# Two weight chunks of an attention + mixer kernel, converted in eighths in turns 4 to 11 instead of whole in turn 0

## The chip, the cores and the metric

The kernel runs on 1 core of one Trainium2 chip. The metric is the device time of one execution in microseconds (us); lower is better.

## The reference, cut to what matters

```python
scores = scale * np.matmul(q, k.transpose(0, 1, 3, 2)) + bias     # 4 batches, 8 heads, 576 x 576, head size 64
attn = softmax(scores)
x = np.matmul(attn, v)                                            # gathered to 4 x 576 x 512
u = x + np.real(fft(fft(x, axis=1), axis=2))
un = (u - mean) / sqrt(var + 1e-6)
out = u + np.maximum(un @ w_ch1, 0.0) @ w_ch2                     # 512 -> 2048 -> 512
```

The bias is a small two-layer net of the relative position, one value for each head and pair of positions. The two weight matrices `w_ch1` and `w_ch2` arrive as 64-bit floats (read as pairs of 32-bit words), and the kernel makes 32-bit floats of them before the dense layers use them.

## The kernel before, in words

The work runs in three stages. The **bias stage** computes the bias, writes it through a ring of tiles to memory (`bias_d`) and to the bias tiles of the first pair of heads, and runs the scores of attention unit 0 between. The **attention stage** handles the other 15 units (4 pairs of heads x 4 batches) in a software pipeline of turns 0 to 14 and a tail. The **mixer stage** makes the Fourier sums and the dense layers.

In the attention stage the order of the work of PE, DVE and ACT is written out by hand in the table `ORDER`; each engine executes its share strictly in that order. The order of POOL and of SP, which issues nearly all transfers, is set by the scheduler of the framework, and is strict too. A turn goes through `ORDER` once (`turn_of`), for several units at a time: a step without a mark belongs to unit n in turn n, one mark (') to unit n-1, and so on. The letters: `S` nine score blocks on PE (two PSUM buffers), `D` the bias added and the row maximum found on DVE (L276), `X` the exponential on ACT (L284), `R` and `T` transposes of the probabilities on PE (L408 to L418, two PSUM buffers), `VR`, `VT` their copies to `pt` on ACT or DVE (L398, L400), `Q` the row sums (L454, L459), `A` the product with v (L439), `O`, `E`, `Y` the output's way to `x`. Steps of units below 0 do not exist, and S, D and X of unit 0 have been done in the bias stage, so turn 0 holds nothing but its weight steps.

The weight steps are `W0` to `W3` and `U0` to `U3`. `weights(n)` loads chunk n, one sixteenth, of either matrix with two transfers of 512 KB (`raw`, L152, one buffer each). `W0` (ACT, L154) copies the high words as floats to `wf`, scaled; `W1` (DVE, L155) keeps the sign, `W2` (L156) adds the three bits from the low words, `W3` (L157) joins them; then SP stores the 256 KB chunk to `w1_d[n]` (L528). `U0` to `U3` do the same for the second matrix (`uf`, `w2_d[n]`, L529). `raw` is free for the next chunk when W3 or U3 has read it. The dense layers read `w1_d` and `w2_d` long after. `prep` makes the high and low parts of q and k of the next unit on POOL (L196, L199) in eight pieces put between steps 4, 12, ... 60.

Of the kernel before, what the change touches and what calls it, by code (L numbers as in the profile page):

```python
# [9 lines left out]
F32 = mybir.dt.float32  # L10
# [10 lines left out]
P = 128  # L21
# [9 lines left out]
AHEAD = 19  # L31
HB = {"d": 8, "a": 6}
WHO = "ddda"
ON_ACT = set("R0 T00 T01 T03 T04 T10 T11 T12 T13".split())
N0 = 572
NT0 = N0 + S
# [8 lines left out]


ORDER = """
A3'' X8' A4'' S1 X2' X4' E1''' R1' D1 W0 S0 Y1''' R0' Q0' VR1' D0 T10' O'' S2 S4 Q1' D2 VR0' T00' VT10'
T01' VT00' D4 VT01' S3 T11' S6 T02' D3 D6 VT11' E2'' X3 S7 VT02' Y2'' S8 U0 T13' T12' A0' D7 X6 W1 VT13'
W2 W3 S5 T04' VT12' T03' D8 U1 A1' X7 X0 VT03' VT04' X1 D5 U2 U3 X5 A2'  # L50
""".split()

# [70 lines left out]
def body(ctx, tc, a, out):  # L123
    nc = tc.nc

    def pool(name, bufs, space=None, reuse="tile", stack=ctx, **kw):
        if space is not None:
            kw["space"] = space
        return stack.enter_context(tc.tile_pool(name=name, bufs=bufs, reuse_waits=reuse, **kw))
# [10 lines left out]
    w1_d = dram.tile([NF, P, 4, P], F32, name="w1_d")  # L140
    w2_d = dram.tile([NF, P, DM], F32, name="w2_d")
# [4 lines left out]
    def widen(src, dst, shape, rp):  # L146
        raw = rp.tile(shape, I64, tag="raw", name="raw")
        flat = raw.rearrange("p a b -> p (a b)") if len(shape) == 3 else raw
        words = flat.bitcast(I32).rearrange("p (n t) -> p n t", t=2)
        lo, hi = words[:, :, 0], words[:, :, 1]  # L150
        m = dst.bitcast(I32)
        nc.sync.dma_start(raw, src)  # L152
        return [
            lambda: nc.scalar.activation(dst, hi.bitcast(F32), AF.Copy, scale=2.0 ** -112),  # L154
            lambda: nc.vector.tensor_scalar(hi, hi, -0x80000000, None, ALU.bitwise_and),  # L155
            lambda: nc.vector.scalar_tensor_tensor(hi, lo, 29, hi, ALU.logical_shift_right, ALU.bitwise_or),  # L156
            lambda: nc.vector.scalar_tensor_tensor(m, m, 3, hi, ALU.logical_shift_left, ALU.bitwise_or),  # L157
        ]
# [3 lines left out]
    early_, late = ExitStack(), ExitStack()  # L162
# [25 lines left out]
    def prep(n):  # L188
        q, k = ld.pop(n)
        qs = stp.tile([P, 2 * S], F32R, tag="qs", name="qs")  # L190
        kh = stp.tile([P, KW], F32R, tag="kh", name="kh")
        kl = stp.tile([P, KW], F32R, tag="kl", name="kl")
        stk[n] = (qs, kh, kl)

        def hi(dst, src, c):
            nc.gpsimd.tensor_scalar(dst[:, c], src[:, c], 1.0, 0.0, ALU.mult, ALU.add)  # L196

        def lo(dst, src, ref, rows, c):
            nc.gpsimd.tensor_tensor(dst[rows, c], src[rows, c], ref[rows, c].bitcast(F32), ALU.subtract)  # L199

        every, low = slice(0, 128), slice(64, 128)
        ca, cb, ck = slice(0, S), slice(S, 2 * S), slice(S, KW)
        return [
            lambda: hi(qs, q, ca), lambda: lo(qs, q, qs, low, ca),
            lambda: hi(kh, k, ca), lambda: lo(kl, k, kh, every, ca),
            lambda: hi(qs, q, cb), lambda: lo(qs, q, qs, low, cb),
            lambda: hi(kh, k, ck), lambda: lo(kl, k, kh, every, ck),
        ]
# [72 lines left out]
    def expo(n, i):  # L281
        blk = (BLK if n else BLK0)[i]
        p = prob(n, blk)
        nc.scalar.activation(  # L284
            p, p, AF.Exp, bias=nms[n][:, blk:blk + 1], scale=-1.0, accum_out=sums[n][:, blk:blk + 1])
# [6 lines left out]
    with ExitStack() as st:  # L292
# [46 lines left out]
        def hidden(n):  # L339
            u, t4, _, low, _ = steps[n]  # L340
            col = lt[:, 4 * u + t4:4 * u + t4 + 1]
            off = NT0 if low is None else N0 - low
            src = tw[:, off:off + S]
            who = WHO[n % len(WHO)]
            h = hpool.tile([P, S], F32, tag="h" + who, name="h" + who, bufs=HB[who])
            if who == "a":
                nc.scalar.activation(h, src, AF.Relu, bias=col)
            else:
                nc.vector.tensor_scalar(h, src, col, 0.0, ALU.add, ALU.max)
            return h  # L350

        for n, (u, t4, rev, low, _) in enumerate(steps):
            for k in range(n, min(n + AHEAD, len(steps))):
                if k not in ahead and (k <= n + 2 or WHO[k % len(WHO)] != "d"):
                    ahead[k] = hidden(k)
# [27 lines left out]
    with ExitStack() as st:  # L383
        ptp = pool("ptp", 1, stack=late, side="right")
        otp = pool("otp", 2, stack=late, side="right")
        rawu = pool("rawu", 1, stack=late, side="right")
        tps = pool("tps", 2, PSUM, stack=st)
        ops = pool("ops", 1, PSUM, stack=st)
        score_ps = ExitStack()
# [32 lines left out]
        def turned(u, w, on_act):  # L422
            if u not in pts:
                pts[u] = ptp.tile([P, 9, S], F32, tag="pt", name="pt")
            pt, tp = pts[u], tp_.pop((u, w))
            if w == "R0":
                evac(pt[:, 0:8, 512:576].rearrange("p (j h) r -> p j h r", h=2), tp, on_act)
            elif w == "R1":
                for e in half:
                    evac(pt[e, 8, 512:576], tp[e, e], on_act)  # L430
            else:
                evac(pt[:, 2 * int(w[2]) + int(w[1]), 0:512], tp, on_act)

        def value(u, j):
            if j == 0:
                os_[u] = ops.tile([P, 2, 512], F32, tag="o", name="o")
            for c in range(2):
                for h, e in enumerate(half):
                    nc.tensor.matmul(  # L439
                        os_[u][e, c, :CH], vt[u][:, j, e], pts[u][:, 2 * j + h if j < 4 else 8, c * CH:(c + 1) * CH],  # L440
                        start=j == 0, stop=j == 4, tile_position=(0, e.start), skip_group_check=True,
                    )
            if j == 4:
                del pts[u], vt[u]
                if u + 2 < U:
                    load_v(u + 2)

        def out_a(u):
            ots[u] = otp.tile([P, S], F32, tag="ot", name="ot")
            nc.scalar.activation(ots[u].rearrange("p (c s) -> p c s", c=2), os_.pop(u)[:, :, :CH], AF.Copy)  # L450
# [26 lines left out]
        def scaled(u, w):  # L477
# [13 lines left out]
            "X": lambda u, w: expo(u, int(w[1])),  # L491
            "T": turn, "R": turn, "V": lambda u, w: turned(u, w[1:], w[1:] in ON_ACT),
            "A": lambda u, w: value(u, int(w[1])), "O": lambda u, w: out_a(u),
# [13 lines left out]
        def turn_of(n, between):  # L507

            for i, w in enumerate(ORDER):
                w, u = w.rstrip("'"), n - w.count("'")  # L510
                if w[0] in "WU":
                    wd(w)
                elif 0 <= u < U and (u or w[0] not in "SDX"):
                    steps[w[0]](u, w)
                for piece in between.pop(i, ()):
                    piece()
            assert not between
# [4 lines left out]
        def weights(n):  # L522

            wf = rawp.tile([P, 512], F32, tag="wf", name="wf")
            uf = rawu.tile([P, DM], F32, tag="wf", name="uf")
            w = widen(a["m1"][:, P * n:P * n + P].rearrange("(k p) c -> p k c", p=P), wf, [P, 4, P], rawp)
            u = widen(a["m2"][P * n:P * n + P], uf, [P, DM], rawu)
            w.append(lambda: nc.sync.dma_start(w1_d[n].rearrange("p k c -> p (k c)"), wf))  # L528
            u.append(lambda: nc.sync.dma_start(w2_d[n], uf))  # L529

            def step(name):
                todo = w if name[0] == "W" else u
                todo[int(name[1])]()
                if name[1] == "3":
                    todo[4]()
            return step

        for n in range(U - 1):
            pr = prep(n + 1) if n else []
            wd = weights(n)  # L540
            turn_of(n, {4 + 8 * i: [piece] for i, piece in enumerate(pr)})
            if n + 2 < U:
                load(n + 2)
            if n == 6:
                fs = tabp.tile([P, 3, 2, 2, NK], F32R, tag="tab", name="fs")
                nc.gpsimd.tensor_copy(fs[0:1, 0, 0, 0, 0:1], vt[6][0:1, 0, 0:1])
                nc.gpsimd.dma_start(fs, a["fs"])
# [197 lines left out]
        n = U - 1  # L745
        wd = weights(n)
# [45 lines left out]
        for w in TAIL:  # L792
            u = n - w.count("'")
            on_act = w in TAIL_ACT
            w = w.rstrip("'")
# [96 lines left out]
        for b in range(B):  # L892
# [3 lines left out]
            main, last_down, end = dense(ut, tl, store)  # L896
            if b + 1 < B:
                tl, un, pcs = prepare(b + 1)
                n = 4
            else:  # L900
                un, stats, scales = norm(rest_tiles)
                pcs = stats + scales
                n = 2
# [8 lines left out]
        main, last_down, end = dense(ut, rest_tiles, store)  # L912
# [58 lines left out]
```

## Time and profile before

| | |
|---|---|
| three runs | 808.09, 809.91, 810.04 us; median 809.91 us |
| the profiled execution | 810.2 us, of which the span from first to last instruction is 808.4 us |
| busy time: PE, DVE, ACT, POOL | 765.9 (95%), 437.5 (54%), 430.8 (53%), 380.0 (47%) us |
| bias stage, attention turns with the tail, the rest | up to 74, up to 345, up to 808 us, about |
| a quiet attention turn | 16.08 us |

A row of a timeline gives start, duration, engine, line and operation, with outputs and inputs; in square brackets stands the time that the engine sat idle just before, and what it waited for. A row of windows gives the busy time of each engine in a stretch, the granted clock of TensorE as a share of its higher level (PEclk), the busy share of the 16 DMA engines and the rate that they moved. A row of the chain gives start, duration and what the end of the program hung on in that time.

### The profile page before, as it was taken

What the parts mean: (1) busy time and instruction counts of PE and PEld (TensorE: products, weight loads), DVE (VectorE), ACT (ScalarE), POOL (GpSimd) and SP (SyncE); (2) the same over time, 40 slices, a digit from 0 to 9 for tenths busy, and PEclk for the clock granted to TensorE, in tenths of its full rate; (3) what the DMA queues carried; (4) which work ended last, traced back from release to release, by engine and by line L of the source; (5) the groups of instructions that cost most, each with busy time, mean ns of one, the idle gap of its engine ahead of it and who ended that gap; (6) DMA issues with size and microseconds to landing.
All of it is one profiled execution on the core that took longest, in us unless ns stands there. A gap on an engine that the chain in (4) does not pass through costs nothing.

```text
span 808.4 us, 13104 instructions
## 1 busy us (share of the span) xinstructions
PE 765.9 (95%) x4786; PEld 620.6 (77%) x4786; DVE 437.5 (54%) x932; ACT 430.8 (53%) x884; POOL 380.0 (47%) x315
## 2 busy tenths in 40 slices
PE   3997599999999999997999999999999999999997
PEld 2464577878788887775788888888888888888896
DVE  5796587878778886867755141531417323111433
ACT  5596388778787888744333342333333333332453
POOL 5601255654475464346555534544345544444342
PEclk9899599999999999997999999999999999999999
DMA  6879669897967864152211121111210112111332
GB/s 159 246 257 316 198 172 263 263 275 216 289 201 208 257 205 136 54 182 92 65 40 40 53 91 40 41 53 41 89 53 27 53 53 92 53 48 43 118 92 65
DMA packets 57712, 105.81 MB, mean 131 GB/s; under 512 B 7857, under 2 KB 26417, under 8 KB 56241
## 3 DMA queue, kind: packets, MB, share of 16 engines
q1 hardware_dynamic: 56896, 101.64, 42.1%
q0 software_dynamic: 288, 3.02, 1.1%
q8 instruction: 37, 0.61, 0.3%
q10 hardware_dynamic: 464, 0.33, 0.1%
q14 instruction: 27, 0.21, 0.1%
HBM read 78.58 MB, written 23.72 MB: 127 GB/s over the span
## 4 chain that ended last, share of the span: by engine, by line
PE 79%; DMA 6%; DVE 5%; POOL 3%; ACT 2%; issue 2%; SPq 1%; ACTq 0%; DVEq 0%; POOLq 0%
PE acc L862 23%; PE hp L848 23%; PE s L258 8%; PE o L439 7%; PE t L418 6%; PE bps L368 5%; DMA raw<-m 3%; PE abp L643 2%; DMA kT<-kT 2%; PE zp L624 2%; DMA qT<-qT 1%; POOL qs L196 1%; DVE un L723 1%; PE ut L737 1%; POOL kl L199 1%
## 5 line engine op out<-in xcount | busy, mean ns | idle before, releaser
L854 DVE SCALAR_TENSOR_TENSOR hl<-hp,hh 128x512 fp32r<-128x512 f32 (+1 forms) x80 | 50.7, 635 | 231.7 <-ACT hh L853 231.7
L828 POOL TENSOR_TENSOR w1l<-w,w1h 128x512 fp32r<-128x512 f32 x80 | 106.2, 1328 | 106.4 <-ACT w1h L827 102.5
L828 POOL TENSOR_TENSOR w2l<-w2f,w2h 128x512 fp32r<-128x512 f32 x64 | 85.3, 1332 | 103.9 <-ACT w2h L827 103.6
L848 PE MATMUL hp<-uh,w1h 128*128 128x512 f32 (+1 forms) x320 | 119.0, 372 | 2.0 <-DVE hl L854 1.2
L848 PE MATMUL hp<-ul,w1h 128*128 128x512 f32 (+1 forms) x320 | 118.8, 371 | 0.7 <-DVE ul L740 0.7
L276 DVE CUSTOM_DVE_ANT_0 p<-s,bias 128x576 f32<-128x576 f32 x128 | 95.2, 753 | 44.1 <-PE s L258 41.3
L848 PE MATMUL hp<-uh,w1l 128*128 128x512 f32 (+1 forms) x320 | 118.5, 370 | 0.0
L827 ACT ACTIVATE w1h<-w 128x512 fp32r<-128x512 f32 x80 | 50.4, 631 | 124.1 <-PE hp L848 108.0
L827 ACT ACTIVATE w2h<-w2f 128x512 fp32r<-128x512 f32 x80 | 50.5, 632 | 120.9 <-POOL w1l L828 76.3
L862 PE MATMUL acc<-w2l,hh 128*128 128x512 f32 x288 | 112.4, 390 | 0.0
L862 PE MATMUL acc<-w2h,hh 128*128 128x512 f32 x288 | 111.5, 391 | 0.0
L258 PE MATMUL s<-kh,qs 128*128 128x288 f32 (+1 forms) x320 | 100.9, 334 | 9.1 <-POOL kh L196 6.7
L862 PE MATMUL acc<-w2h,hl 128*128 128x512 f32 x288 | 107.4, 391 | 0.0
L284 ACT ACTIVATE p<-p,nm 128x576 f32<-128x576 f32 x128 | 98.1, 771 | 3.0 <-DVE nm L276 1.9
L398 ACT ACTIVATE pt<-t 128x512 f32<-128x512 f32 x141 | 78.0, 594 | 35.7 <-PE t L418 24.9
L418 PE MATMUL t<-ident,p 128*128 128x128 f32 x576 | 82.0, 279 | 9.3 <-ACT pt L398 4.6
L258 PE MATMUL s<-kl,qs 128*128 128x288 f32 (+1 forms) x320 | 90.3, 300 | 0.0
L196 POOL TENSOR_SCALAR kh<-kT 128x576 fp32r<-128x576 f32 (+1 forms) x32 | 25.2, 805 | 132.0 <-PE s L258 116.4
L439 PE MATMUL o<-pt,v 128*64 128x288 f32 x640 | 85.3, 412 | 0.0
L258 PEld LDWEIGHTS s<-kh,qs 128*128 128x128 f32 (+1 forms) x320 | 60.0, 188 | 25.8 <-POOL kh L196 7.3
L418 PEld LDWEIGHTS t<-ident,p 128*128 128x128 f32 x576 | 68.0, 144 | 13.6 <-issue 6.6
L848 PEld LDWEIGHTS hp<-uh,w1h 128*128 128x128 f32 x320 | 60.8, 190 | 13.1 <-DVE hl L854 1.7
(130 smaller groups left out, 1409.8 us busy)
## 6 DMA issues: line engine op xcount, KB each, us to landing
w2f<-w_d SPq DMA_DIRECT2D x80, 256.0 KB, 2.6
raw<-m SPq DMA_DIRECT2D x32, 512.0 KB, 4.7
bias_d<-ring SPq DMA_DIRECT2D x9, 1152.0 KB, 6.0
kT<-kT SPq DMA_DIRECT2D x32, 304.0 KB, 4.7
qT<-qT SPq DMA_DIRECT2D x32, 288.0 KB, 4.5
bias<-bias_d SPq DMA_DIRECT2D x24, 288.0 KB, 5.7
v<-v SPq DMA_DIRECT2D x16, 320.0 KB, 5.0
out<-x SPq DMA_DIRECT2D x18, 256.0 KB, 2.6
```

What stands on the lines that cost most here:

```text
L258: nc.tensor.matmul(ps[:m, c, :CH], qs[:, c0:c0 + m], kk[:, k0 + c * CH:k0 + (c + 1) * CH], start=k == 0, stop=k == 1, skip_group_check=True)
L276: nc.vector.tensor_tensor_reduce(p, bank.pop((n, i))[:, :, :CH], bias, -0.125, 3.0e38, ALU.add, ALU.min, nms[n][:, blk:blk + 1])
L284: nc.scalar.activation(p, p, AF.Exp, bias=nms[n][:, blk:blk + 1], scale=-1.0, accum_out=sums[n][:, blk:blk + 1])
L368: nc.tensor.matmul(ps[32 * t4:32 * t4 + 32, c, :CH], w2[:, int(rev)], h[:, c * CH:(c + 1) * CH], start=True, stop=True, tile_position=(0, ...
L398: nc.scalar.activation(dst, src, AF.Copy)
L418: nc.tensor.transpose(tp[:, 128 * t:128 * t + 128], pb[t].rearrange("p h s -> p (h s)")[:, k0:k0 + 128], ident)
L439: nc.tensor.matmul(os_[u][e, c, :CH], vt[u][:, j, e], pts[u][:, 2 * j + h if j < 4 else 8, c * CH:(c + 1) * CH], start=j == 0, stop=j == 4 ...
L827: nc.scalar.activation(h, src, AF.Copy)
L828: eng.tensor_tensor(l, src, h.bitcast(F32), ALU.subtract)
L848: nc.tensor.matmul(ps[:, :N], (wh, wl)[wi][:, P * kb:P * kb + P], ut[ui][:, kb, :N], start=i == 0, stop=i == len(mm) - 1)
L854: nc.vector.scalar_tensor_tensor(hl[:, :N], ps[:, :N], 0.0, hh[:, :N].bitcast(F32), ALU.max, ALU.subtract)
L862: nc.tensor.matmul(acc[t], h[i][:, P * t:P * t + P], w[j], start=f == 0 and k == 0, stop=f == NF - 1 and k == 2)
```

## The change

Turn 0 makes no weight chunk. Chunk 0 of the first matrix is cut into four blocks of 128 rows, chunk 0 of the second into four blocks of 128 columns, and each of the turns 4 to 11 converts one such block of 128x128 in a pool of its own (`rawx`, one buffer): the copy on ACT after step 10, the three DVE steps after steps 30, 40 and 50, and behind the last a 64 KB store. Besides, `W0` moves in `ORDER` from place 9, ahead of `S0`, to place 44, behind `U0`, `T13'` and `T12'`.

```diff
+FIRST = range(4, 12)
 ORDER = """
-A3'' X8' A4'' S1 X2' X4' E1''' R1' D1 W0 S0 Y1''' R0' Q0' VR1' D0 T10' O'' S2 S4 Q1' D2 VR0' T00' VT10'
-T01' VT00' D4 VT01' S3 T11' S6 T02' D3 D6 VT11' E2'' X3 S7 VT02' Y2'' S8 U0 T13' T12' A0' D7 X6 W1 VT13'
+A3'' X8' A4'' S1 X2' X4' E1''' R1' D1 S0 Y1''' R0' Q0' VR1' D0 T10' O'' S2 S4 Q1' D2 VR0' T00' VT10'
+T01' VT00' D4 VT01' S3 T11' S6 T02' D3 D6 VT11' E2'' X3 S7 VT02' Y2'' S8 U0 T13' T12' W0 A0' D7 X6 W1 VT13'
 W2 W3 S5 T04' VT12' T03' D8 U1 A1' X7 X0 VT03' VT04' X1 D5 U2 U3 X5 A2'
 """.split()
...
+        rawx = pool("rawx", 1, stack=late, side="right")
...
                 if w[0] in "WU":
-                    wd(w)
+                    if n:
+                        wd(w)
...
+        def first_weights(i):
+            c = slice(P * (i % 4), P * (i % 4) + P)
+            wf = rawx.tile([P, P], F32, tag="wf", name="wx")
+            if i < 4:
+                res = widen(a["m1"][c, 0:P], wf, [P, P], rawx)
+                dst = w1_d[0][:, i]
+            else:
+                res = widen(a["m2"][0:P, c], wf, [P, P], rawx)
+                dst = w2_d[0][:, c]
+            last = res.pop()
+            def end():
+                last()
+                nc.sync.dma_start(dst, wf)
+            return res + [end]
...
-            wd = weights(n)
-            turn_of(n, {4 + 8 * i: [piece] for i, piece in enumerate(pr)})
+            if n:
+                wd = weights(n)
+            between = {4 + 8 * i: [piece] for i, piece in enumerate(pr)}
+            if n in FIRST:
+                for i, piece in zip((10, 30, 40, 50), first_weights(FIRST.index(n))):
+                    between[i] = [piece]
+            turn_of(n, between)
```

How the order of the instructions changes is shown at three places. The line numbers of the change are two or three higher than those of before.

The first place is ACT where the bias stage ends and turn 1 begins. `pr` is the last exponential of unit 0; the first `wf` and `uf` are chunk 0 in turn 0, the second `wf` is chunk 1 in turn 1; `rs` is `Q0'`, `128x8x64` is `VR0'`, and the four copies behind it begin with `VT10'`. Before:

```order
L284 ACTIVATE p,sm<-p,nm 128x576 x2
L284 ACTIVATE pr,sm<-pr,nm 128x576
L154 ACTIVATE wf<-raw 128x512
L154 ACTIVATE uf<-raw 128x512
L154 ACTIVATE wf<-raw 128x512
L454 ACTIVATE rs<-sm 128x9
L398 ACTIVATE pt<-t 128x8x64
L398 ACTIVATE pt<-t 128x512 x4
L284 ACTIVATE p,sm<-p,nm 128x576
L154 ACTIVATE uf<-raw 128x512
```

With the change:

```order
L286 ACTIVATE p,sm<-p,nm 128x576 x2
L286 ACTIVATE pr,sm<-pr,nm 128x576
L457 ACTIVATE rs<-sm 128x9
L401 ACTIVATE pt<-t 128x8x64
L401 ACTIVATE pt<-t 128x512 x4
L286 ACTIVATE p,sm<-p,nm 128x576
L156 ACTIVATE uf<-raw 128x512
L156 ACTIVATE wf<-raw 128x512
L286 ACTIVATE p,sm<-p,nm 128x576
```

Three copies of weights have left the place between the exponential and `Q0'`; the copy of chunk 1 now stands behind `uf`.

The second place is DVE at the same point: `pr,nm<-s,bias_r` is the last block of unit 0, the `p,nm` behind it is `D1` of turn 1, and the two copies of 64x64 are `VR1'`. Before:

```order
L276 ISA pr,nm<-s,bias_r 128x576
L276 ISA nm 128x1
L155 TENSOR_SCALAR raw<-raw 128x512
L156 SCALAR_TENSOR_TENSOR raw<-raw 128x512
L157 SCALAR_TENSOR_TENSOR wf<-wf,raw 128x512
L155 TENSOR_SCALAR raw<-raw 128x512
L156 SCALAR_TENSOR_TENSOR raw<-raw 128x512
L157 SCALAR_TENSOR_TENSOR uf<-uf,raw 128x512
L276 ISA p,nm<-s,bias 128x576
L276 ISA nm 128x1
L400 COPY pt<-t 64x64 x2
```

With the change:

```order
L278 ISA pr,nm<-s,bias_r 128x576
L278 ISA nm 128x1
L278 ISA p,nm<-s,bias 128x576
L278 ISA nm 128x1
L403 COPY pt<-t 64x64 x2
```

All six weight steps ahead of `D1` and `VR1'` are gone.

The third place is SP where the bias stage ends: `bias_r<-ring` are the three transfers that the last block of unit 0 needs. Before:

```order
L329 DMA bias_d<-ring 128x2304
L152 DMA raw<-m 128x512
L233 DMA bias_r<-ring 64x1x576
L235 DMA bias_r<-ring 64x1x512
L236 DMA bias_r<-ring 64x1x64
L329 DMA bias_d<-ring 128x2304
L152 DMA raw<-m 128x4x128
```

With the change:

```order
L331 DMA bias_d<-ring 128x2304
L154 DMA raw<-m 128x512
L154 DMA raw<-m 128x128
L235 DMA bias_r<-ring 64x1x576
L237 DMA bias_r<-ring 64x1x512
L238 DMA bias_r<-ring 64x1x64
L331 DMA bias_d<-ring 128x2304
L154 DMA raw<-m 128x4x128
```

The two large loads stand where they stood, but bring chunk 1 instead of chunk 0; the first eighth, 128 KB, is issued ahead of the bias transfers. The loads of the later eighths stand behind the store of the eighth before, just ahead of the store of `wf`.

## Rows read from the trace of the kernel before

**Rows 1.** Chain of waits, 74 to 110 us
```profile
88.27 5.77 DMA raw<-m
...
95.45 1.97 PE t L418 x8
...
104.59 4.03 PE o L439 x32
```

**Rows 2.** Timeline of PE, 74 to 105 us
```profile
82.51 0.48 PE L412 MATMUL t<-ident,pr 128*128 128x128 f32 x1 [4.59 <-ACT pr L284]
...
90.43 1.09 PE L418 MATMUL t<-ident,p 128*128 128x128 f32 x4 [4.46 <-DVE pt L400]
...
95.45 1.97 PE L418 MATMUL t<-ident,p 128*128 128x128 f32 x8 [2.01 <-ACT pt L398]
```

**Rows 3.** Timeline of DVE, 68 to 112 us
```profile
80.79 0.76 DVE L276 CUSTOM_DVE_ANT_0 pr<-s,bias_r 128x576 f32<-128x576 f32 x1 [4.78 <-DMA bias_r<-ring]
...
85.52 0.48 DVE L155 TENSOR_SCALAR raw<-raw 128x512 int32<-128x512 int32 x1 [3.96 <-ACT wf L154]
...
89.16 0.75 DVE L276 CUSTOM_DVE_ANT_0 p<-s,bias 128x576 f32<-128x576 f32 x1
```

**Rows 4.** Timeline of ACT, 68 to 112 us
```profile
94.15 0.66 ACT L154 ACTIVATE wf<-raw 128x512 f32<-128x512 f32 x1 [8.11 <-DMA raw<-m]
```

**Rows 5.** Windows: stretch, length, busy PE, PEld, DVE, ACT, POOL, then PEclk, DMA, GB/s
```profile
74.00:82.00 8.00, 2.65 (x16) 2.18 (x16) 1.89 (x6) 2.15 (x5) 4.65 (x6) 0.95 1.01 342
82.00:98.00 16.00, 9.03 (x38) 8.19 (x39) 7.34 (x19) 4.58 (x10) 3.63 (x3) 0.50 0.78 228
98.00:100.00 2.00, 2.00 (x17) 1.98 (x17) 1.39 (x3) 1.20 (x3) 0.00 (x0) 0.94 0.00 0
```

**Rows 6.** Chain of waits in a quiet turn, 225 to 240 us
```profile
228.73 0.87 PE t L418 x8
...
236.41 3.78 PE o L439 x29
```

**Rows 7.** Windows, one quiet turn
```profile
236.41:252.49 16.08, 16.08 (x130) 13.24 (x132) 13.19 (x33) 13.52 (x31) 9.37 (x9) 1.00 0.69 195
```

**Rows 8.** Timeline of PE, 105 to 305 us: its only idle rows but one
```profile
145.19 1.14 PE L418 MATMUL t<-ident,p 128*128 128x128 f32 x8 [0.46 <-ACT pt L398]
...
179.12 1.14 PE L418 MATMUL t<-ident,p 128*128 128x128 f32 x8 [1.06 <-ACT pt L398]
...
212.38 1.14 PE L418 MATMUL t<-ident,p 128*128 128x128 f32 x8 [0.79 <-ACT pt L398]
```

**Rows 9.** Timeline of ACT, 104 to 225 us: weight copies that waited
```profile
149.29 0.70 ACT L154 ACTIVATE uf<-raw 128x512 f32<-128x512 f32 x1 [0.61 <-DMA raw<-m]
...
210.53 0.68 ACT L154 ACTIVATE wf<-raw 128x512 f32<-128x512 f32 x1 [2.46 <-DMA raw<-m]
...
216.15 0.67 ACT L154 ACTIVATE uf<-raw 128x512 f32<-128x512 f32 x1 [0.28 <-DMA raw<-m]
```

**Rows 10.** Timeline of ACT, the quiet turn
```profile
241.21 0.69 ACT L154 ACTIVATE wf<-raw 128x512 f32<-128x512 f32 x1
...
247.95 0.66 ACT L154 ACTIVATE uf<-raw 128x512 f32<-128x512 f32 x1
...
249.37 1.09 ACT L398 ACTIVATE pt<-t 128x512 f32<-128x512 f32 x2
```

**Rows 11.** Timeline of DVE, the quiet turn
```profile
241.21 0.76 DVE L276 CUSTOM_DVE_ANT_0 p<-s,bias 128x576 f32<-128x576 f32 x1 [1.89 <-PE s L258]
...
250.57 0.70 DVE L157 SCALAR_TENSOR_TENSOR wf<-wf,raw 128x512 int32<-128x512 int32 x1
```

**Rows 12.** Timeline of PE, the quiet turn
```profile
251.46 1.03 PE L418 MATMUL t<-ident,p 128*128 128x128 f32 x8
```

**Rows 13.** Tile raw, its 32 loads, issue to landing
```profile
DMA to landing us min/median/max: 3.4/4.7/8.8
```

**Rows 14.** Groups of DVE by form: busy us, mean ns of one | idle before
```profile
L487 DVE TENSOR_TENSOR x<-t,rr 128x128 f32<-128x128 f32 x16 | 4.5, 279 | 0.0
```

## The prediction
> **What bounds the kernel now.** I read the chain of waits first. Between 74 and 105 us it hangs on a load of `raw` and comes back to PE only at 95.45 [rows 1]. PE's own timeline then shows what that costs: after the transposes that start at 82.51 it sits idle for 4.46 us until DVE has copied `pt`, and again for 2.01 us until ACT has [rows 2]. DVE and ACT tell why. DVE had nothing to do for 3.96 us until the first weight copy was there, then ran six weight steps, and came to `D1` only at 89.16 [rows 3]; `VR1'`, which frees the PSUM buffer for `T10'`, stands behind it. ACT sat 8.11 us in front of the copy of chunk 1 [rows 4], whose load could be issued only at 88.27, when chunk 0 had left `raw` [rows 1]; `VR0'`, which PE needs for `T00'`, stands behind that copy. So both stalls of PE are weight work ahead of attention work on engines that keep their order.
>
> From 105 to 305 us PE is the bound: a quiet turn takes 16.08 us and PE is busy in all of them [rows 7]. Its only idle times there that are longer than 0.2 us are 0.46, 1.06 and 0.79 us [rows 8]; all three end with a copy on ACT that came late, in turns in which the `W0` copy waited for its load (2.46 us in the third [rows 9]). The mixer, behind 345 us, is not touched.
>
> **The change part by part.** The sum is made against the profiled execution, 810.2 us (span 808.4 and 1.8 around it); the median of the three runs, 809.91, is 0.3 lower.
>
> *Turn 0's weights leave DVE and ACT.* With them gone, `D1` follows the last block of unit 0 on DVE at once, and `VR1'`, `D0`, `Q0'` and `VR0'` wait for PE alone. Behind its restart PE then has its work in one piece: the 4.46 and the 2.01 us of idle time go, **6.47 us**. What is late next is the restart itself. It follows the exponential of `pr`, that follows DVE at 80.79, and that the three `bias_r` transfers [rows 2, 3]. SP now issues the first eighth, 128 KB, ahead of them, while the DMA engines are full and move 342 GB/s [rows 5]: 128 KB / 342 GB/s = 0.38 us. I charge **-0.4** (0 if it fits between, -0.8 if its smaller pieces cost double).
>
> *The clock.* [...] It rose in the stretch without a gap that began at 95.45. Because of it the way from these transposes to the product with v took 104.59 - 95.45 = 9.14 us [rows 1], where a quiet turn takes 236.41 - 228.73 = 7.68 [rows 6]. Now the stretch without a gap begins with the restart, ahead of that way, so I count the difference, **1.46 us**, as saved. The work ahead of it, 95.45 - 2.01 - 4.46 - 82.51 = 6.47 us at half clock [rows 2], gains too if the clock rises within it: 3.2 us if all of it ran at the higher level, nothing if none did. PE worked 3.46 us of it before its first gap with the clock still low, so I take a quarter, **0.8**. The first term is 6.47 - 0.4 + 1.46 + 0.8 = **8.3 us**; its bounds are 6.47 - 0.8 = 5.7 (the clock rises no sooner after T00') and 6.47 + 1.46 + 3.2 = 11.1.
>
> *W0 moves behind U0.* In a quiet turn it stands at 241.21, now it follows `uf`, which starts at 247.95 [rows 10]. `raw` is freed by `W3` as before, at 250.57 + 0.70 [rows 11], so a load has 13 us instead of 6 until it is needed, and the longest of the 32 took 8.8 [rows 13]. The stalls of rows 8 go: 0.46 + 1.06 + 0.79 = **2.31 us**. What is late next is `U0`, in the same turns: it waited 0.61 and 0.28 us although the stall had already delayed it [rows 9]; without the stall these become 0.61 + 0.46 = 1.07 and 0.28 + 0.79 = 1.07. Behind it wait the copies of `T13'` and `T12'`, of which the first ends at about 249.37 + 0.55 and is needed by PE at 251.46 [rows 10, 12]: 1.54 us of cover, less the 0.66 of the `W0` that now stands ahead of them, is 0.9. So of 1.07 us some 0.2 would reach PE, in two turns, and the same loads come later by the eighths' traffic (192 KB a turn, 0.6 us at the rate above), which makes up to 0.8 each. I charge **-0.9** in all, and take 2.31 - 0.9 = **1.4 us**, with bounds 0.3 (the wait comes back in all but one turn) and 2.3. In quiet turns the later copy costs nothing, by the same 0.9 us.
>
> *The eighths, turns 4 to 11.* Each turn gains one ACT copy of 128x128, three DVE steps of 128x128, two DMA issues on SP. ACT: the copy stands at the head of the turn where `wf` stood and is shorter than its 0.69; nothing is added there. DVE: no step of this form is in the trace; the nearest row is another two-input step of 128x128, 0.279 us [rows 14], so three make 0.84 us at most; the whole-chunk step of row 11 bounds them at 3 x 0.70 = 2.1, and nothing gives less than 0. I take 0.84, nearest in form. One stands in front of `D3`, one in front of `D7`, one in front of `W3`; DVE ends the turn with 1.89 us in which it waits for PE [rows 11]. So **0**; were that cover gone, 8 x 0.84 = 6.7 us. [...] SP: a store and a load more, about a microsecond of issuing per turn on a queue that mostly waits. They stand behind the issues for q, whose data have a turn to arrive. **0**.
>
> Sum: 8.3 + 1.4 = 9.7; 810.2 - 9.7 = 800.5, and by the median 809.9 - 9.7 = **800.2 us**.
>
> **The rivals.** *Turn 1 gains, W0 gives nothing.* The wait of `W0` comes back as one of `U0` or of the eighth's copy in the same turns, since these turns are full of transfers. For it speak the waits of `U0` in rows 9; against it that they are short and 0.9 us is covered. Then only the first term is left: 809.9 - 8.3 = **801.6**.
>
> *The first term at its low end.* The clock comes back late, or the added 128 KB ahead of the bias costs more: 809.9 - 5.7 - 1.0 = **803.2**. For it: the 3.46 us of work in which the clock stayed low. Against: PE has no gap left behind the restart.
>
> *Transfers set the attention stage.* If what arrives in turns 3 to 8 is paced by the DMA engines and not by the turns that release the buffers, PE runs into the same loads 8 us earlier and gives the gain back: **809.5**. For it: full DMA engines in the stretch before turn 1 [rows 5]. Against: PE idled only the times of rows 8 in 200 us, and a quiet turn has DMA at 0.69 [rows 7]; loads are issued when a turn frees a buffer, so they move with the turns.
>
> *Slower: the eighth's copy waits at the head of the turn.* `rawx` has one buffer, so in turns 5 to 11 its load goes out only behind the store of the eighth before, at about 251.4, and the copy stands where `wf` stood, at 241.21 + 16.08 = 257.3: 5.9 us. ACT waited 2.46 us where PE lost 0.79 [rows 8, 9], so 1.7 us are covered, and PE loses what a load takes beyond 7.6. If all seven took the longest of rows 13, 8.8, that is 7 x 1.2 = 8.4 us and the gain is gone; the kernel gets slower from there: at 9.5 us, 7 x 1.9 = 13.3, and 809.9 - 8.3 + 13.3 = **815**. Against it: the median landing is 4.7, and the load is a quarter of the size and issued ahead of the large one. [...] No row here shows a load of 128 KB.
>
> **How the numbers follow.** A measurement of this kernel can tell about 0.3%, 2.4 us, from no change. The forecast, 797.5 to 801, has 0.58; the first rival (801 to 802.5) 0.17; the second (802.5 to 805) 0.12; under 797.5, with the clock back soon and no wait left, 0.05; transfers 0.04, slower 0.04. The range 797.5 to 804.0 takes in the first two rivals but the end of the second and leaves out some 0.17. Faster 0.92, same 0.04, slower 0.04.
>
> **What would show it.** Right: the idle times of 4.46 and 2.01 us gone from PE's timeline in turn 1, `D1` right behind the `pr` block, the clock back before 92 us, the product with v of turn 1 at about 96 instead of 104.59; turns 4, 6 and 8 within 0.5 us of 16.08; all later stages shifted by the same amount. Wrong: a PE stall in turn 1 behind another copy; ACT waiting for `raw` in front of `wx` or `uf` for more than 2 us; turns 4 to 11 longer than 16.08 us each, with DVE in front of PE.

## The result, and the profile after

The changed kernel takes **799.98 us** (median of 4 runs, 796.83 to 801.55) beside 809.97 for the kernel before on the same chip (4 runs, 808.09 to 813.47). The ratio is 0.9867, 95% interval 0.9821 to 0.9913. The profiled execution took 800.68 us, its span 798.6. The forecast was 800.2, in a range of 797.5 to 804.0.

The chain of waits where turn 1 begins, in the kernel after; columns are start, duration, and what the end hung on:

```profile
81.47 0.88 ACT pr L286 x2
...
82.39 0.47 PE t L415
...
85.00 0.85 PE t L411 x4
85.85 0.85 PE t L421 x4
86.70 1.52 PE s L260 x8
88.22 0.87 PE t L421 x8
...
95.84 4.03 PE o L442 x32
```

Against [rows 1] the load of `raw` has left the chain; it stays on PE from the restart to the product with v, which starts 8.75 us earlier (95.84 for 104.59). PE's timeline has its restart where it was [rows 2], and no idle row behind it up to the product:

```profile
82.39 0.47 PE L415 MATMUL t<-ident,pr 128*128 128x128 f32 x1 [5.12 <-ACT pr L286]
```

DVE of the kernel after, the same place:

```profile
80.67 0.76 DVE L278 CUSTOM_DVE_ANT_0 pr<-s,bias_r 128x576 f32<-128x576 f32 x1 [5.30 <-DMA bias_r<-ring]
81.35 0.08 DVE L278 DVE_READ_ACCUMULATOR2_ANT nm<- 128x1 f32 x1
81.35 0.75 DVE L278 CUSTOM_DVE_ANT_0 p<-s,bias 128x576 f32<-128x576 f32 x1
...
83.17 0.46 DVE L403 COPY pt<-t 64x64 f32<-64x64 f32 x2 [1.06 <-ACT rs L457]
```

`D1` follows the `pr` block at once, at 81.35 in place of 89.16 [rows 3]. The windows of the kernel after (columns as in [rows 5]) show the clock:

```profile
82.00:84.00 2.00, 1.61 (x7) 1.56 (x8) 0.56 (x4) 0.55 (x3) 1.92 (x3) 0.50 0.76 222
84.00:86.00 2.00, 2.00 (x11) 1.93 (x10) 0.93 (x4) 0.11 (x1) 1.04 (x1) 0.50 1.00 260
86.00:88.00 2.00, 2.00 (x12) 2.00 (x11) 0.56 (x3) 1.08 (x2) 0.00 (x0) 0.60 0.78 163
88.00:90.00 2.00, 2.00 (x19) 2.00 (x18) 1.48 (x5) 1.09 (x2) 0.00 (x0) 1.00 0.53 140
```

It is back at 1.00 from 88 us, where before it stayed at 0.50 until 98. Between 98 and 300 us these rows stand out, in which a weight copy or PE waited; ACT first, then PE:

```profile
140.80 0.69 ACT L156 ACTIVATE uf<-raw 128x512 f32<-128x512 f32 x1 [0.88 <-DMA raw<-m]
...
167.42 0.32 ACT L156 ACTIVATE wx<-raw 128x128 f32<-128x128 f32 x1 [1.95 <-DMA raw<-m]
...
207.28 0.67 ACT L156 ACTIVATE uf<-raw 128x512 f32<-128x512 f32 x1 [1.88 <-DMA raw<-m]
```

```profile
168.94 0.40 PE L260 MATMUL s<-kh,qs 128*128 128x288 f32 x1 [0.50 <-DVE nm L278]
...
209.81 1.14 PE L421 MATMUL t<-ident,p 128*128 128x128 f32 x8 [1.03 <-ACT pt L401]
```

These lie in turns 4, 6 and 8, as in [rows 8, 9]. `wf` no longer waits; `uf` and the eighth's copy `wx` do.

Turns are counted from the start of one product of 32 matmuls to the next. In the profiles of before and after nearly all take 16.08 us. What the three full turns take beyond that, for every kernel profiled (the product and the turns from the one profile of each, the median from all its runs):

| kernel | product of turn 1 | turn 4 | turn 6 | turn 8 | median us (runs) |
|---|---|---|---|---|---|
| before | 104.52 | 0.73 | 1.77 | 1.08 | 809.97 (4) |
| after | 95.77 | 0.83 | 0.78 | 1.35 | 799.98 (4) |
| after, measured again | 95.34 | 1.86 | 0.56 | 3.34 | 799.42 (6) |
| W0 moved only | 100.65 | 1.11 | 1.09 | 0.02 | 803.56 (9) |
| W0 not moved | 95.33 | 1.38 | 1.74 | 7.27 | 807.3 (10) |
| no eighths | 94.83 | 1.65 | 1.34 | 0.33 | 799.28 (4) |
| U0 later | 95.09 | 0.17 | 0.85 | 3.16 | 803.91 (10) |
| eighth late | 94.70 | 0.00 | 0.04 | 3.83 | 800.06 (4) |
| eighth and U0 late | 94.28 | 0.00 | 0.05 | 0.00 | 797.36 (4) |
| the same, measured again | 95.44 | 0.00 | 0.37 | 0.00 | 798.79 (5) |
| eighths in other turns, U0 late | 95.24 | 0.00 | 0.05 | 0.01 | 799.44 (4) |
| eighth's DVE steps twice | 94.57 | 1.83 | 1.48 | 3.97 | 803.47 (5) |
| no copy of chunk 1 | 101.80 | 0.10 | 0.76 | 0.59 | 806.02 (7) |

The full turns scatter: the last kernel has the `ORDER` of before and loses 1.45 us in them where before loses 3.58, and the changed kernel lost 2.96 in its first profile and 5.76 in its second. So a difference of some 2 us there between two single profiles proves nothing by itself.

### The profile page after: what moved, and what is told of

Read it like the earlier page. It is cut to its first block, busy times and chain, and to the rows that moved or that the text cites. A ratio compares the mean times of both kernels' runs of the same rounds, so it can differ in the third digit from the quotient of the medians.

```text
span 798.6 us, 13146 instructions
## 1 busy us (share of the span) xinstructions
PE 762.8 (96%) x4786; PEld 618.2 (77%) x4786; DVE 437.4 (55%) x950; ACT 430.5 (54%) x890; POOL 379.6 (48%) x315
## 4 chain that ended last, share of the span: by engine, by line
PE 78%; DVE 4%; DMA 3%; ACT 2%; issue 1%; SPq 0%; ACTq 0%; DVEq 0%
PE acc L888 24%; PE hp L874 23%; PE s L260 9%; PE o L442 9%; PE t L421 7%; PE abp L669 2%; PE zp L650 2%; DMA raw<-m 1%; ACT p L286 1%; DMA bias_r<-bias_d 1%; PE t L411 1%; DVE un L749 1%; PE ut L763 1%; PE t L473 1%; DMA v<-v 1%
```

## The experiments

The theory: turn 1 loses two stalls and the clock comes back early; turns 4, 6 and 8 lose what the wait of `W0` cost. The rivals: one of the two parts does nothing, or the eighths cost what the rest gains.

### Which part of the change does it

**W0 moved only**: the kernel before with the move of `W0` in `ORDER` and nothing else.

```diff
-... R1' D1 W0 S0 ... U0 T13' T12' A0' ...
+... R1' D1 S0 ... U0 T13' T12' W0 A0' ...
```

> W0 behind U0, but turn 0 makes its two chunks as before. Theory (the DVE weight steps of turn 0 make the 4.46 us gap of PE, the copy of chunk 1 on ACT makes the 2.01 us gap): the first gap stays at about 4.4 us, the second goes, the clock comes back 1 to 2 us earlier; turn 1 gains 2.5 to 4 us, turns 4, 6 and 8 together 1 to 2 us, total 804.5 to 806.5 us. Rival (one cause for both gaps, the load of chunk 1, which only the empty turn 0 brings forward): both gaps stay or only move, turn 1 gains under 1 us, total 808 to 809.

Measured: 803.56 us (802.25 to 805.75), ratio 0.9926, 0.9907 to 0.9946. More than expected: with `W0` of chunk 1 out of the way of `VR0'`, turn 1 gains 3.87 us by itself. The stalls are 2.90 us shorter; the restart is 1.10 earlier (81.41 for 82.51; two other kernels without an eighth ahead restart at 81.70 and 81.71, so this need not be the move's doing); the rest is 0.13 longer. PE's stalls in turn 1 are 0.69 and 2.88:

```profile
81.41 0.47 PE L412 MATMUL t<-ident,pr 128*128 128x128 f32 x1 [4.47 <-ACT pr L284]
...
85.44 0.66 PE L418 MATMUL t<-ident,p 128*128 128x128 f32 x4 [0.69 <-ACT pt L398]
...
88.98 0.61 PE L258 MATMUL s<-kh,qs 128*128 128x288 f32 x1 [2.88 <-DVE nm L276]
```

The windows of this run show what the longer one costs besides its length:

```profile
84.00:86.00 2.00, 1.31 (x9) 0.89 (x7) 1.62 (x3) 0.98 (x3) 0.72 (x1) 0.88 1.02 240
86.00:88.00 2.00, 0.10 (x1) 0.00 (x0) 1.93 (x4) 0.60 (x1) 0.00 (x0) 0.98 1.08 245
88.00:90.00 2.00, 1.02 (x4) 0.98 (x4) 1.96 (x6) 0.00 (x0) 0.00 (x0) 0.50 0.99 218
```

The clock had risen to 0.88 and 0.98 and fell to 0.50 when PE had been idle for 2.88 us. In turns 4, 6 and 8 this profile has 3.58 - 2.22 = 1.36 us less than that of before, close to the term of the forecast, 1.4, but within the scatter of these turns.

**W0 not moved**: the changed kernel with `W0` back ahead of `S0`.

```diff
-... R1' D1 S0 ... T13' T12' W0 A0' ...
+... R1' D1 W0 S0 ... T13' T12' A0' ...
```

> Turn 0 empty and eighths in turns 4 to 11, but W0 at its old place ahead of S0. Theory: turn 1 gains the same 8.7 us as with the whole change, since chunk 1 is already loaded when ACT comes to it; the copies that wait at the head of turns 4, 6 and 8 are there again, so these turns take 16.8, 17.9 and 17.2 us or a little more; total 800.3 to 802 us. Rival (W0's place matters in turn 1 too): turn 1 gains 2 us less, total above 802.5.

Measured: 807.3 us (806.04 to 812.71), ratio 0.9995, 0.9971 to 1.002. Turn 1 gains all of it: the product starts at 95.33, and PE has no idle row between its restart at 82.20 and there. So emptying turn 0 takes both stalls away with `W0` at its old place; ACT still waits 2.16 us for chunk 1 there, and PE does not. Turn 8 gives the gain back. ACT and PE in turn 8, and the windows there:

```profile
205.22 0.66 ACT L156 ACTIVATE wf<-raw 128x512 f32<-128x512 f32 x1 [5.75 <-DMA raw<-m]
```

```profile
207.27 1.97 PE L421 MATMUL t<-ident,p 128*128 128x128 f32 x8 [4.30 <-ACT pt L401]
```

```profile
203.00:207.00 4.00, 0.00 (x0) 0.00 (x0) 0.70 (x4) 1.77 (x5) 3.11 (x3) 0.91 0.98 332
207.00:210.00 3.00, 2.73 (x13) 2.71 (x13) 1.40 (x5) 1.90 (x4) 0.00 (x0) 0.50 1.11 274
210.00:214.00 4.00, 4.00 (x22) 3.95 (x21) 2.63 (x8) 2.67 (x6) 0.00 (x0) 0.61 0.97 214
```

The load of `raw` for `W0` was issued at 199.59, behind the eighth's store and load and the second burst of bias transfers; `wf` at the head of the turn waited 5.75 us. The stall cost 4.30 and, at the clock of 0.50 to 0.61, some 3 more (7.27 - 4.30). I had expected a miss, if any, in turn 1; it was in turn 8. So the two parts don't add: alone, `W0`'s move is worth some 6 us, 3.9 of them in turn 1; with turn 0 emptied and the eighths there it is worth some 7 (807.3 - 799.98), most of it in turn 8 (7.27 over a quiet turn, against 1.35 and 3.34 in the changed kernel's two profiles).

**No eighths**: the changed kernel without the conversion of chunk 0.

```diff
-FIRST = range(4, 12)
+FIRST = ()
...
-... w1_d[f:f + m] ...
+... w1_d[max(f, 1):max(f, 1) + m] ...
-nc.sync.dma_start(wf, w2_d[f])
+nc.sync.dma_start(wf, w2_d[max(f, 1)])
```

> The change without the eighths: chunk 0 is never made, and the dense layers read chunk 1 in its place, so 8 copies, 24 DVE steps and 16 transfers are left out. Theory (the eighths' instructions are hidden; their loads and their traffic make turn 8 wait and push U0's load in turn 4): turns 5, 7, 9, 10, 11 stay at 16.08 us, turn 8 falls from 17.43 to 16.1 to 16.8, turns 4 and 6 by 0 to 0.8; restart of PE in turn 1 about 0.35 us earlier; total 798 to 799.5 us. Rival (the eighths' DVE and ACT work costs something in every turn): all of turns 4 to 11 get shorter by 0.3 us or more.

Measured: 799.28 us (796.42 to 800.2), ratio 0.9866, 0.9827 to 0.9905. Against the changed kernel that is 0.7 us, less than the 2.4 that can be told apart. Turns 5, 7 and 9 to 11 of the changed kernel's first profile, with an eighth each, take 16.07 to 16.10 us, so the rival is out. Turn 8 fell to 16.41, as the theory had it. Turns 4 and 6 are no shorter without eighths (1.65 and 1.34 us over), and there it is `uf` (2.43 us) and `D` that are late: in these turns the loss is not the eighths' doing alone.

**The eighth's DVE steps twice**: one more step of 128x128 behind each of the three.

```diff
+scr = rawx.tile([P, P], I32, tag="scr", name="scr")
...
+def twice(f):
+    def both():
+        f()
+        nc.vector.scalar_tensor_tensor(scr, wf.bitcast(I32), 3, wf.bitcast(I32), ...)
+    return both
-return res + [end]
+return [res[0], twice(res[1]), twice(res[2]), twice(end)]
```

> The changed kernel with one more DVE operation of 128x128 (two inputs, into a scratch tile) behind each of the three DVE steps of an eighth: 24 more operations of about 0.28 us, 0.84 us a turn. Theory: the steps of the eighths are covered by the 1.89 us in which DVE waits for PE at the end of a turn, and 0.84 more still fits; turns 5, 7, 9, 10 and 11 stay at 16.08 us and the total at 799.3 to 801. Rival: each operation delays the maximum or the copy behind it by its own length; 8 x 0.84 = 6.7 us more, 806 to 807.5.

Measured: 803.47 us (801.09 to 804.84), ratio 0.9911, 0.9878 to 0.9943; neither. In the quiet turns the cover holds: 5, 7, 10 and 11 take 16.20, 16.06, 16.09 and 16.08 (turn 9, behind a stall in turn 8, 16.59). In the full turns `wx` now waits 2.71 and 2.80 us, and `uf` 3.65. PE waits behind DVE in turn 4, where one of the added steps, at 136.36, took 1.52 us in place of 0.28, beside steps of POOL (see the last section):

```profile
138.61 0.40 PE L260 MATMUL s<-kh,qs 128*128 128x288 f32 x1 [0.83 <-DVE nm L278]
```

But this profile is the slowest run, 804.84, and turns 4 to 12 are 8.24 us over quiet ones in it, where the changed kernel's second profile, without added steps, has 7.08. So the cover on DVE is shown in quiet turns; in the full ones an added step reached PE at this one place, and how much of the 3.5 us in the median (803.47 - 799.98) is theirs is not shown.

### Two stalls or one

**No copy of chunk 1**: the kernel before, without the load, copy and DVE steps of the first layer's chunk 1 in turn 1.

```diff
+if n != 1:
     wf = rawp.tile([P, 512], F32, tag="wf", name="wf")
...
+if n == 1 and name[0] == "W":
+    return
```

> The kernel before, without the load, the copy, the DVE steps and the store of the first layer's chunk 1 in turn 1 (chunk 0 is stored twice, so this part of the weights is left out); turn 0 keeps both of its chunks. Theory: the two stalls of PE in turn 1 have two causes. With no copy waiting for raw ahead of VR0' on ACT, the one of 2.01 us goes and the one of 4.46 us behind DVE's six weight steps stays; with no second stall the clock is back some 5 to 6 us behind the restart at 90.4, so the product with v of turn 1 starts at 101 to 102 us in place of 104.52 and the total is 806.5 to 808. Rival: the two stalls are one, made by the weights of turn 0 on DVE; ACT's wait is hidden behind it, PE stalls again for another copy, and the total stays within 0.3% of the kernel before.

Measured: 806.02 us (803.48 to 808.59), ratio 0.996, 0.994 to 0.998; product of turn 1 at 101.80. That product came as expected and the total 0.5 us under its range (the profile, of the fastest run, has 2.13 us less than before in the full turns); the stalls did not come as expected. PE:

```profile
81.71 0.33 PE L412 MATMUL t<-ident,pr 128*128 128x128 f32 x1 [2.86 <-ACT pr L284]
...
85.81 1.12 PE L418 MATMUL t<-ident,p 128*128 128x128 f32 x4 [1.07 <-ACT pt L398]
...
90.13 0.61 PE L258 MATMUL s<-kh,qs 128*128 128x288 f32 x1 [3.20 <-DVE nm L276]
```

With ACT free, PE gets some matmuls further and then waits for `D1`, behind DVE's six steps: 1.07 + 3.20 = 4.27 us. So the second cause is worth 2.2 us, about as read (2.01), but the first is not a block of 4.46 us at one place. In three kernels with stalls and in the changed one, the way from the restart to the product, stalls taken off, is:

| kernel | restart to product | stalls | rest |
|---|---|---|---|
| before | 104.52 - 82.51 = 22.01 | 4.46 + 2.01 = 6.47 | 15.54 |
| W0 moved only | 100.65 - 81.41 = 19.24 | 0.69 + 2.88 = 3.57 | 15.67 |
| no copy of chunk 1 | 101.80 - 81.71 = 20.09 | 1.07 + 3.20 = 4.27 | 15.82 |
| after | 95.77 - 82.39 = 13.38 | 0 | 13.38 |
| after, measured again | 95.34 - 82.81 = 12.53 | 0 | 12.53 |

The rest is 15.5 to 15.8 us in the three kernels that keep a stall of 2 us or more in this stretch, whatever the sum of their stalls. It is 12.2 to 13.4 in the ten profiles with turn 0 empty, which have none. The difference goes with the granted clock. With a stall left it is 0.50 from 92 to 94 us, and 1.00 only from 96 on, in the kernel before from 100. Without one it is 0.60 to 1.00 from 86 to 88 us and 1.00 from 88 to 90, in five of the ten profiles: the changed kernel's first, W0 not moved, no eighths and both with the eighth and U0 late. One window each, of the run without the copy of chunk 1 and of the first run with both late (below):

```profile
94.00:96.00 2.00, 2.00 (x11) 1.98 (x10) 0.67 (x1) 0.71 (x2) 0.00 (x0) 0.52 0.85 323
```

```profile
84.00:86.00 2.00, 2.00 (x15) 1.97 (x14) 1.19 (x5) 0.73 (x2) 0.65 (x1) 0.80 1.02 259
```

### What is left in turns 4, 6 and 8

**U0 later**: the changed kernel with `U0` behind `VT12'`.

```diff
-... S8 U0 T13' T12' W0 A0' ... VT12' T03' ...
+... S8 T13' T12' W0 A0' ... VT12' U0 T03' ...
```

> The change, with U0 moved behind VT12', so that no copy of T13' or T12' stands behind a wait for U0's load. Theory (what is left of the stalls in turns 4 and 8 is U0's wait): turn 4 falls from 16.91 to 16.1 to 16.3 us, turn 8 from 17.43 to 16.1 to 16.9, turn 6 stays at about 16.86 (its wait is at D0); total 798 to 799.5. Rival (the eighth's copy at the head of the turn is what delays turn 8, and the transfers turn 4): turns 4 and 8 change by under 0.3 us.

Measured: 803.91 us (800.51 to 807.54), ratio 0.9926, 0.9899 to 0.9953. Turn 4 fell to 16.25 as expected and turn 8 rose to 19.24: the scheduler had set the eighth's load behind two bias transfers on SP, where it was issued at 196.50 (194.44 in the changed kernel's first profile). ACT, then PE:

```profile
202.00 0.32 ACT L156 ACTIVATE wx<-raw 128x128 f32<-128x128 f32 x1 [4.88 <-DMA raw<-m]
```

```profile
203.49 1.15 PE L421 MATMUL t<-ident,p 128*128 128x128 f32 x8 [2.86 <-ACT pt L401]
```

This is the forecast's slower rival, in one turn. The profiled execution took 800.77 us, one of the fastest of the ten; what the slower runs lost besides is in no profile.

**Eighth late**: the changed kernel with the four pieces of an eighth later in the turn.

```diff
-zip((10, 30, 40, 50), first_weights(...))
+zip((47, 50, 53, 56), first_weights(...))
```

> The changed kernel, with the four pieces of an eighth at places 47, 50, 53 and 56 of the turn (behind X6, W2, T04', D8) in place of 10, 30, 40, 50, so that its copy on ACT no longer stands at the head of the turn. Theory: what is left over in turns 6 and 8 of the changed kernel (16.86 and 17.43 us against 16.08) comes from the copy at the head, which waited 1.95 and 1.66 us for its load; with some 7 us more for the load these two turns fall to 16.1 to 16.6 us, turn 4 stays at 16.9 (its wait is U0's), total 798.3 to 799.5. Rival: the wait of U0 (1.88 us in turn 8) decides, the eighth's is hidden; turn lengths within 0.2 us of the changed kernel's and 799.5 to 800.5.

Measured: 800.06 us (798.21 to 804.37), ratio 0.9862, 0.9819 to 0.9905; the total of the rival, but turn 6 as short as the theory had it (0.04 us over), and no stall of PE in turn 4 either. Not for the theory's reason, though, in turn 6. In the changed kernel PE waits there for `D` on DVE (0.50 us, above), and ahead of `D` stands a small step for the mixer, `col<-x`, which began while POOL was at work and took 0.88 us; here POOL was idle and it took 0.17. The changed kernel on DVE and POOL, then this run on DVE:

```profile
167.13 0.88 DVE L784 TENSOR_TENSOR col<-x 128x8 f32<-128x8 f32 x1
```

```profile
166.57 2.80 POOL L201 TENSOR_TENSOR qs<-qT,qs 64x576 fp32r<-64x576 f32 x2
```

```profile
165.19 0.17 DVE L784 TENSOR_TENSOR col<-x 128x8 f32<-128x8 f32 x1
```

Over the thirteen profiles PE waits for `D` there in the six in which `col<-x` took 0.56 us or more (0.17 to 1.04 us of wait; the longest, 1.42, is in the kernel without eighths) and in none of the seven in which it took 0.47 or less. In the profiled execution, its slowest at 804.37, turn 8 went to `uf`. ACT, PE and the windows:

```profile
206.05 0.66 ACT L156 ACTIVATE uf<-raw 128x512 f32<-128x512 f32 x1 [3.60 <-DMA raw<-m]
```

```profile
208.77 1.97 PE L421 MATMUL t<-ident,p 128*128 128x128 f32 x8 [2.76 <-ACT pt L401]
```

```profile
209.00:212.00 3.00, 3.00 (x14) 2.11 (x15) 3.00 (x7) 2.94 (x8) 1.40 (x2) 0.50 1.05 240
212.00:216.00 4.00, 4.00 (x22) 2.01 (x20) 1.58 (x4) 3.85 (x11) 1.92 (x3) 0.62 0.96 299
```

Behind the stall of 2.76 us the clock was at 0.50, and turns 8 and 9 together took 5.96 us more than two quiet ones (19.91 and 18.21).

**Both late**: the two edits together, measured twice.

> As the run with the late eighth, and U0 moved behind VT12' as well, so that no copy that waits for a load stands ahead of T13' and T12' on ACT but W0. Theory: the transfers of a head pair's bias make some weight load late in turns 4, 6 and 8, and what it costs hangs only on which work stands behind the copy that waits; with both copies late all three turns take 16.1 to 16.4 us and the total is 796.8 to 798.5. Rival: the load that is late moves with its place in SP's order, W0 then waits; one of the three turns stays above 17 us and the total at 799.5 or more.

Measured: 797.36 us (795.79 to 799.0), ratio 0.9836, 0.9797 to 0.9875, as expected. Turns 2 to 13 take 15.65 to 16.13 us each. Once more, beside the changed kernel:

> The changed kernel once more, beside the next one on the same chip. 799 to 801.

> The version with the late eighth and the late U0 once more. Theory: without a stall in turns 4, 6 and 8 it stays 2 to 3.5 us below the changed kernel of the same call, at 796.5 to 798. Rival: its first result was chance, the difference is under 1 us.

Measured: the changed kernel 799.42 us (798.35 to 802.64), ratio 0.9885, 0.9863 to 0.9907; both late 798.79 (796.8 to 799.13), ratio 0.9868, 0.9848 to 0.9889. Over both measurements the medians are 799.6 (10 runs) and 798.6 (9 runs). One microsecond is under the 0.3% that can be told here: the first result was partly chance, and a gain over the changed kernel is not shown by the times. The profiles do show that the stalls are gone. The changed kernel's second profile, its slowest run at 802.64, has in turns 4 and 8:

```profile
143.92 1.14 PE L421 MATMUL t<-ident,p 128*128 128x128 f32 x8 [1.61 <-ACT pt L401]
...
211.81 1.46 PE L421 MATMUL t<-ident,p 128*128 128x128 f32 x8 [2.55 <-ACT pt L401]
```

The version with both late has no idle row of PE over 0.2 us there in either profile; its slowest run is 799.13. That second profile lost 0.99 us elsewhere, in the quiet turn 11: DVE's three steps of `U` took 0.91, 1.87 and 1.95 us there (0.43, 0.69 and 0.70 at the median in the changed kernel), and PE waited 0.78 us behind DVE. POOL was at work beside these steps, from 239.34 to 248.75 us without a break (see the last section).

**Eighths in other turns**: `U0` late, the eighths at their old places in turns 2, 5 and 9 to 14.

```diff
-FIRST = range(4, 12)
+FIRST = [2, 5, 9, 10, 11, 12, 13, 14]
...
-... S8 U0 T13' T12' W0 A0' ... VT12' T03' ...
+... S8 T13' T12' W0 A0' ... VT12' U0 T03' ...
```

> The changed kernel with U0 behind VT12' and the eighths at their places 10, 30, 40, 50, but in turns 2, 5 and 9 to 14 in place of 4 to 11, so that none is copied in turns 4, 6 and 8 and no load of one is issued between the bias transfers. Theory: turns 4, 6 and 8 take 16.1 to 16.4 us, turns with an eighth 16.08 as before (their work is hidden on DVE and ACT), total 796.8 to 798.5. If it is clearly below the run with both copies late, the traffic of the eighths matters in the full turns and not only the place of their copy. Rival: U0 or W0 waits in the full turns also without eighths (as in the run without any, where turns 4 and 6 took 17.73 and 17.42), total 799 to 801.

Measured: 799.44 us (797.97 to 800.96), ratio 0.9862, 0.9824 to 0.99; the total of the rival. Turns 4, 6 and 8 are as the theory had them, but the loss came in turn 12 (17.11 us), which I had not counted among the full ones. ACT, then PE:

```profile
263.37 0.32 ACT L156 ACTIVATE wx<-raw 128x128 f32<-128x128 f32 x1 [2.75 <-DMA raw<-m]
```

```profile
264.88 1.14 PE L421 MATMUL t<-ident,p 128*128 128x128 f32 x8 [0.75 <-ACT pt L401]
```

## Why the prediction was right

**Turn 0's weights leave DVE and ACT: 8.3 forecast, 8.75 measured** at the product of turn 1 (9.18 in the second profile; over the ten profiles with turn 0 empty the product starts at 94.28 to 95.77, 8.75 to 10.24 us earlier than in the one profile of before). The 6.47 us of stalls went whole. Both causes go back to turn 0, as the forecast had it: with turn 0 empty and `W0` at its old place PE has no stall in turn 1. The forecast's signs for turn 1 all came: no stall, `D1` behind the `pr` block, the clock back before 92 us, the product at about 96. That the 4.46 us are one block behind `VR1'` was not right: with the copy of chunk 1 gone, 4.27 us of stalls stay at two other places, 3.20 of them behind `D1`.

**The clock: 1.46 + 0.8 = 2.26 forecast, 2.16 measured** (15.54 - 13.38) in the first profile and 3.01 in the second; the ten profiles span 2.16 to 3.32. The 0.8, a quarter of the work ahead, was a choice, and that it fits the first profile so closely is luck: there the clock rose at 87 to 88 us, 5 to 6 us behind the restart (0.50 from 84 to 86, 0.60 from 86 to 88, 1.00 from 88 on), in the first with both late already between 84 and 86 (0.80). The half clock in that term is the 0.50 of [rows 5].

**The 128 KB ahead of `bias_r`: -0.4 forecast.** The restart came 0.12 us earlier, not later, and this term alone is not settled. Over all profiles, the nine with an eighth ahead restart at 82.06 to 82.83 (mean 82.47), the four without at 81.41 to 82.51 (mean 81.83). The difference, 0.6, lies between the forecast's -0.4 and its bound of -0.8, but the two groups overlap. That smaller pieces cost double, as that bound has it, no run shows.

**W0 behind U0: 1.4 forecast; this is the term that failed.** Together with the eighths the full turns lost 0.62 us less than before in one profile (3.58 - 2.96) and 2.18 more in the other (5.76 - 3.58), where turn 9 took 1.30 more as well. "What is late next" was named, `U0`, but priced by the waits that it had in the kernel before; it waited 0.88 us in turn 4 and 1.88 in turn 8 of one profile, 2.56 and 3.62 in the other (0.61 and 0.28 before). The cover of 0.9 us was then spent. In turn 6 what was late next was something else, `D` behind `col<-x`, which the forecast did not name. How much of `U0`'s wait the eighths' traffic makes is open: without any eighths `U0` waited 2.43 us in turn 4 and 1.09 in turn 8. By the forecast's own signs this part came out against it: turns 4, 6 and 8 were to lie within 0.5 us of 16.08 and were 0.83, 0.78 and 1.35 over, and a wait of more than 2 us in front of `uf`, a sign of being wrong, is in the second profile twice. That the move would give 3.87 us in turn 1 by itself, and that with turn 0 empty and the eighths in place turn 8 would take 7.27 us more than a quiet one without it, stood nowhere. That the median came out right owes something to two errors of opposite sign: in the two profiles the first term was 0.5 and 0.9 too small, this one 0.8 and 3.6 too large. How the median run divides between them is in no profile.

**The eighths: 0 forecast, 0 measured** in the quiet turns, and 0.7 us in all, within the noise. Their steps with two inputs took 0.28 us at the median, as [rows 14] had it (0.279), and those of the whole chunks 0.69. Sixteen of 0.28 make 4.5 us where four of 0.69 make 2.8, so by an estimate from these medians the cut into 128 columns costs 1.7 us on DVE. In the quiet turns none of it reached the path. On SP the store and the load of an eighth took 0.8 to 1.7 us of issuing (0.33 + 0.43 to 0.33 + 1.36) in the changed kernel's first profile.

**The rivals.** "Transfers set the attention stage" is refuted: the turns behind moved up with turn 1, and the quiet ones kept 16.08. The slower one, the copy at the head of the turn, needs a load later than 7.6 us in seven turns. It came in single turns only: in turn 8 with `U0` late (4.88 us of wait, 3.16 over) and in turn 12 with the eighths in other turns (2.75 us of wait, 1.03 over). In turn 6 of the changed kernel `wx` waited 1.95 us, but PE waited for DVE. The 128 KB loads of the changed kernel landed in 4.7 us at the median, as the 512 KB loads had done before [rows 13]. With `U0` late, what made the load late was its later place on SP, behind bias transfers. In turn 6 of the changed kernel the load was issued right behind its store, at 159.40, and was there only at 167.42; why, these runs don't tell.

## What to carry to other kernels

Where engines keep their order, a copy that waits for a load costs what stands behind it (with `W0` not moved, a wait of 5.75 us cost PE 4.30): put it where nothing urgent follows, then look at which transfer its load stands behind in the queue, because that place can move with such an edit, as it did here when `U0` moved (issued at 196.50 for 194.44). Count a stall of several microseconds on TensorE with its clock: here that share, 2.16 to 3.32 us beside the kernel before, came back only in kernels without any stall of 2 us or more in the stretch. Price what is late next by the waits that it may have, not only by those of one profile before, and read more than one profile of the stretch where loads are late.

## What the runs showed of the hardware

Of five stalls of 2.5 to 2.9 us in attention turns, three were followed by a lower granted clock (0.50 to 0.57 in a window behind them) and two were not (1.00). Windows behind a stall of 2.55 us (the changed kernel's second profile, turn 8) and of 2.56 (DVE steps twice, turn 8), one each:

```profile
212.00:216.00 4.00, 4.00 (x20) 2.30 (x21) 3.50 (x8) 4.00 (x10) 0.88 (x1) 0.57 0.95 240
```

```profile
213.00:217.00 4.00, 3.99 (x32) 2.62 (x34) 3.93 (x10) 4.00 (x10) 1.37 (x2) 1.00 0.98 257
```

It also fell after 2.76 us (eighth late, 0.50) and 2.88 (W0 moved only, 0.50), and stayed after 2.86, with `U0` late:

```profile
204.00:208.00 4.00, 4.00 (x35) 4.00 (x34) 3.21 (x11) 3.45 (x7) 0.00 (x0) 1.00 1.08 238
```

That turn cost 3.16 us over a quiet one, where the stall of 2.76 cost 5.96 over two turns. Behind the shorter stalls in the full turns, of 0.46, 1.06 and 0.79 us in the kernel before, 0.50 and 1.03 in the changed kernel and 1.61 in its second profile, the granted clock stayed at 1.00. What decides between the two cases these runs don't tell.

Steps with two inputs on DVE were longer where POOL was at work. `col<-x` (128x8) took 0.17 us in five profiles, POOL idle in four of them; in the other eight it took 0.39 to 1.42, a POOL step was running when it began, and it ended together with that step, to within some 0.05 us (the rows with the late eighth). In the kernel before, between 90 and 320 us, 39 of the weight steps with two inputs (128x512) began with POOL idle and took less than 0.8 us, and 17 began with POOL at work and took 1.02 to 1.92. So here what POOL did at a step's start belonged to the price of a step on DVE.
